# u's products over four token tiles, xh and xl in the place of x tiles 9 to 12

## The chip, the cores and the metric

The kernel runs on one core of a Trainium2 chip. A core has five engines that run beside each other and wait for each other by semaphores: TensorE (PE; its weight loads are shown apart as PEld), VectorE (DVE), ScalarE (ACT), GpSimd (POOL) and SyncE (SP), which here only issues transfers. Transfers run on the core's DMA engines, whichever queue issued them. The metric is the device time of one execution in microseconds, as the median of several runs.

## The reference

Two branches over the same x (2048 tokens of 640 values) are mixed with a gate per token.

```python
g = _sigmoid((x * gate_w).sum(-1, keepdims=True))
# branch A: y = Real(DFT_seq(DFT_hidden(x))), with the matrices as inputs
a = jnp.einsum("bsd,ed->bse", x, dft_hid_re)
b = jnp.einsum("bsd,ed->bse", x, dft_hid_im)
y = jnp.einsum("ts,bse->bte", dft_seq_re, a) - jnp.einsum("ts,bse->bte", dft_seq_im, b)
# branch B: 32 heads pick 2 of 256 experts each, by two lists of 16 scores
q = jnp.einsum("nd,dhc->nhc", xf, w_q)           # w_q: 640 x 32 x 256
s1 = jnp.einsum("nhd,ed->nhe", q[..., :dk], k1)  # and s2 with k2
...                                              # top 2 of each, top 2 of the 4 sums, softmax g
act = _gelu(jnp.einsum("nd,nhkd->nhk", xf, u[top_e]))
out = jnp.einsum("nhk,nhk,nhkd->nd", g, act, v[top_e])
return g_token * y + (1 - g_token) * out
```

## The kernel before, in words

Branch B's gathers are done as dense products: GELU(x u^T) for all 256 rows of u and all tokens, and a matrix of gate weights, expert by token, that is multiplied onto it before the product with v. Keys and w_q are multiplied into one score matrix first (WU holds it, and u behind it). Every fp32 operand is split into a high and a low part (`split`: ScalarE rounds to the high part, VectorE or GpSimd subtracts), and every product is three matmuls (`mm3`, lines 143 to 145: high by high, high by low, low by high).

**Pieces.** The sequence products of branch A are 128 pieces (`seq_piece`): real and imaginary part (w), four chunks of 512 columns (c), 16 token tiles (s). A piece is 15 matmuls: x tile s, split (tile X[s]), by five column blocks, against a 128x512 piece of the DFT matrix, into banks 0 to 4. wf is the loaded piece, WS its split ring of four; loads go out five pieces ahead and splits three. After a chunk's 16 pieces, ScalarE copies the banks to ST (line 246), VectorE multiplies by the token gate (line 217), and the partial goes to DRAM (pd, line 227).

**What stands between the pieces.** A table `then`, filled by `at(n, f)`, lists what follows piece n; the program is written out piece by piece, so this table sets the order on all engines and queues. In pieces 0 to 29 w_q is loaded in 32 loads (`load_wq`, five buffers), multiplied by the keys (`w_part`, line 365) and split. The first partial's stores follow piece 24 (`store_piece`, ScalarE's queue).

**Score steps.** From N0 = 30 on, tokens are taken in eight pairs of token tiles, p = 0 to 7, four `score_step`s each, one between two pieces. xT, loaded into xf, is split into xh and xl (`split_xT`); `sum_xT` forms four sums in place on VectorE (lines 437 to 440), split in `split_sums_xT`. Step 0 makes A (six matmuls, bank 5), then `u_pair` multiplies u by the pair's 256 tokens (30 matmuls of 256 columns, bank 7) and ScalarE takes the GELU into act (line 729), stored at once by SP (line 731). Then ScalarE copies A into bank 7 (Z), and step 1, one piece later, adds products onto it. VectorE finds top scores from `sc` in the background (`topk`, `gates`): a pump emits its instructions in proportion to TensorE's time.

**x tiles.** All 16 split x tiles (640 KB each) stay on chip in phase one. Tiles 0 to 8 are then written to DRAM (xd; `put_x`, AWAY = 9) and fetched for each chunk (`get_x`) during the score steps, into the places of tiles 6 to 8; from piece N1 = 66 on they come back to their own. Behind piece 127 stands the last part, hidden-dimension products with `raw` buffers taken from freed places.

Of the kernel before, what the change touches and what calls it, by code (L numbers as in the profile page):

```python
# [38 lines left out]
KZ = KD + 1  # L39
NSTEP = 7 * KZ  # L40
AHEAD = 5
AWAY = 9
BYPASS = 4
ACCUM_END = NT * (NC + 2) - 4

# [61 lines left out]
def gated_mix_kernel(ctx: ExitStack, tc: tile.TileContext, xT, xn, dreT, dimT, wsre, wsim, wq, kT, uT, vv, gw, out):  # L107
# [20 lines left out]
    def ps_t(shape, dt=F32):  # L128
        return bank(7, shape, dt)
# [6 lines left out]
    def split(f, h, l, eng):  # L136

        nc.scalar.activation(h, f, AF.Copy)  # L138
        eng.tensor_sub(l, f, h.bitcast(F32))  # L139
# [56 lines left out]
    def at(n, f, *args):  # L196
        then.setdefault(n, []).append(lambda: f(*args))
# [63 lines left out]
    p1 = p1_stack.enter_context(tc.tile_pool(name="p1", bufs=1, reuse_waits="tile"))  # L261
    pools = [p1]

    def load_x(s):
        if s < NT:
# [4 lines left out]
    def split_x(s):  # L270

        if s < NT:
            X[s] = big.tile([P, 2, D], F32R, name="X", tag=f"X{s}")
# [32 lines left out]


    warm = nc.const_aps.tensor(1.0, [P, 2 * P], mybir.dt.bfloat16)
    t = ps_t([P, 2 * P])
    for n in range(WARM):  # L310
        nc.tensor.matmul(t, warm[:, :P], warm, start=True, stop=True)  # L311

    split_x(0)
    load_piece(4)
# [105 lines left out]
    def split_xT(p, n):  # L420

        if p < NP:
            if not xs:
                xs.update((t, big.tile([P, 2, KD, P], F32R, name=t, tag=t)) for t in ("xh", "xl"))
            split(xf[p][:, n], xs["xh"][:, n], xs["xl"][:, n], nc.gpsimd)

    SX = {}

# [21 lines left out]
        nc.sync.dma_start(xd[s], X[s].bitcast(F32))  # L450

    def get_x(s, tag):
        X[s] = big.tile([P, 2, D], F32R, name="X", tag=f"X{tag}")
        nc.sync.dma_start(X[s].bitcast(F32), xd[s])

    for s in range(AWAY):
# [73 lines left out]
    def x_part(n, k0, k1):  # L530
        return [[xs[t][:, n, k] for k in range(k0, k1)] for t in ("xh", "xl")]

    def s_part(n):
        return [[t[:, k * P:(k + 1) * P] for k in range(2)] for t in SX[n]]
# [9 lines left out]
    def score_step(p, a):  # L544


        i0, i1 = 2 * p, 2 * p + 1
        copy = lambda o, f: nc.scalar.activation(o, f, AF.Copy)  # L548
        if a == 0:
            AB["A"] = bank(5)  # L550
            products(AB["A"], (x_part(0, 0, 2), w_part2(0, 2, 0)), first=True)
            split_sums_xT(p)
            u_pair(p)
            AB["Z"] = bank(7)
            copy(AB["Z"], AB["A"])
        elif a == 1:
            products(AB["Z"], (x_part(0, 2, 4), w_part2(2, 4, 0)), (x_part(0, 4, 5), w_part2(4, 5, 0)))
            new_sc(i0)
            copy(sc_half(i0, 0), AB["Z"])
            AB["Y"] = bank(6)  # L560
            products(AB["Y"], (s_part(1), t_part(1)), first=True)
            AB["Z"] = bank(7)
            copy(AB["Z"], AB["Y"])
            load_xT(p + 1)
        elif a == 2:
            products(AB["A"], (s_part(2), t_part(2)))
            copy(sc_half(i0, 1), AB["A"])
            products(AB["Z"], (s_part(4), w_part2(2, 4, 1)), (x_part(0, 4, 5), w_part2(4, 5, 1)))
            nc.vector.tensor_add(sc_half(i0, 1), sc_half(i0, 1), AB["Z"])
            bg.credit -= 0.75  # L570
            picks(i0, scs.pop(i0))
            products(AB["A"], (s_part(3), t_part(3)))
            new_sc(i1)
            copy(sc_half(i1, 1), AB["A"])
            split_xT(p + 1, 0)
        else:
            products(AB["Y"], (x_part(1, 4, 5), w_part2(4, 5, 1)))
            nc.vector.tensor_add(sc_half(i1, 1), sc_half(i1, 1), AB["Y"])
            products(AB["A"], (x_part(1, 2, 4), t_part(4)), (x_part(1, 4, 5), w_part2(4, 5, 0)))
# [137 lines left out]
        if i % NB == NB - 1:  # L717
            bg.add(gates(i // NB))

    def u_pair(p):  # L720
        xh, xl = xs["xh"], xs["xl"]
        ps = bank(7, (P, 2, 2 * P))
        for n in range(2):
            c = slice(n * P, (n + 1) * P)
# [4 lines left out]
        nc.scalar.activation(act, ps, AF.Gelu_apprx_tanh)  # L729
# [184 lines left out]
    def split_sums(k):  # L914
        if k == KD:
            f = p3.tile([P, 4 * TC], F32R, name="ts", tag="hot0")
            TS[8] = f[:, :2 * D]
            raw_free.append(f[:, 2 * D:2 * D + TC].bitcast(F32))
            raw_tags.extend((("xf", 2), ("X9", 2)))
        for n in () if k == KD else [k] + ([5 + k // 2] if k % 2 == 0 else []):  # L920
            TS[n] = big.tile([P, 2 * D], F32R, name="ts", tag=f"X{(1, 3, 4, 5, 6, 0, 2, 7)[n]}")
        t = T["t"]
        t1, t5, t3, t6 = (t[:, n * 2 * P:(n + 1) * 2 * P] for n in range(4))
        for n, f in enumerate((t1, t3, t5, t6, t[:, 8 * P:])):
            split(f, t_sum(k, n, 0), t_sum(k, n, 1), nc.gpsimd if n < 2 else nc.vector)
        bg.credit -= 1.0

    def load_v():
        T[KD] = big.tile([P, 2, D], F32, name="dt", tag="X9")
        nc.sync.dma_start(T[KD], vv.rearrange("k p d -> p k d"))  # L930

    def split_v():
# [13 lines left out]
    at(NPC + 14, store_gates, 1)  # L946


    fresh, raw_free = deque(), deque()
    raw_tags = [("X8", 2)] + [("wf", 1)] * 4 + [("X10", 2), ("wf", 1)] + [(f"X{s}", 2) for s in range(11, 16)]  # L950
    raw, sp = {}, {}

    def take(key):
# [305 lines left out]
```

## Time and profile before

| | |
|---|---|
| median of 3 runs | 752.96 us (752.92 to 755.22) |
| the profiled execution | 753.44 us, span 751.7 us |
| TensorE busy | 746.7 us, 4045 matmuls |
| VectorE, ScalarE, GpSimd busy | 587.4, 361.7, 346.6 us |
| granted TensorE clock | 1.000 |
| moved by DMA | 165.89 MB |

Busy time of an engine is the union of its instructions; matmuls overlap, so their pace is read from the starts of successive ones and not from their durations. In the timeline a row is start, duration, engine, line, operation, output and inputs; "x4" merges four, and what stands in brackets is the idle time before it and what ended it. A piece takes 3.40 us of TensorE.

### The profile page before, as it was taken

Reading aid. Unit: us, or ns where it says so; the run is one execution under the profiler, and the core shown is the slowest. Engines: PE = TensorE matmul, PEld = TensorE weight load, DVE = VectorE, ACT = ScalarE, POOL = GpSimd, SP = SyncE. Lnnn points to the kernel's source line nnn. Section 1 sums busy time; section 2 is a strip of 40 time slices with the busy share of each in tenths; the row PEclk is TensorE's granted clock in tenths of the full one; section 3 lists DMA queues with packets and bytes.
Section 4 is the critical chain, followed back from the end, with each engine's and each line's share of the span. In section 5 each row is a group of like instructions: output and inputs, shape, how many; then the busy total and the mean of one; then the engine's idle time right before and its main releaser. Section 6 shows DMA issues by size and latency. Waiting matters only on the chain.

```text
span 751.7 us, 11366 instructions
## 1 busy us (share of the span) xinstructions
PE 746.7 (99%) x4045; PEld 610.7 (81%) x4045; DVE 587.4 (78%) x741; ACT 361.7 (48%) x660; POOL 346.6 (46%) x286
## 2 busy tenths in 40 slices
PE   9999999999999999999999999999999999999998
PEld 7777777888888888888888888888888888888887
DVE  6864088278999999998999888979999983357651
ACT  4334134534345835553734687633555653443451
POOL 5533225342424424334345445643356793487253
PEclk9999999999999999999999999999999999999999
DMA  9999999478366786663496856388766689775301
GB/s 334 378 388 356 342 381 345 132 191 278 57 174 149 184 273 164 159 167 118 121 376 210 175 146 203 116 255 291 264 225 209 218 261 335 228 233 182 112 29 71
DMA packets 84490, 165.89 MB, mean 221 GB/s; under 512 B 16081, under 2 KB 23377, under 8 KB 84177
## 3 DMA queue, kind: packets, MB, share of 16 engines
q1 hardware_dynamic: 70960, 140.89, 55.5%
q0 software_dynamic: 5472, 9.96, 8.6%
q10 hardware_dynamic: 8000, 14.31, 5.2%
q8 instruction: 32, 0.52, 0.3%
q14 instruction: 26, 0.20, 0.1%
HBM read 132.46 MB, written 31.08 MB: 218 GB/s over the span
## 4 chain that ended last, share of the span: by engine, by line
PE 96%; DMA 2%; DVE 2%; issue 0%; SPq 0%; ACT 0%
PE b L143 30%; PE b L144 30%; PE b L145 30%; PE b L239 2%; PE b L365 2%; DMA wq<-in_wq 2%; PE b L815 1%; PE b L311 1%; DVE ST L217 1%; DVE WU L139 0%; DVE tw L139 0%; DVE wp L371 0%; ACT WU L138 0%; DVE tt L397 0%; DVE tt L396 0%
## 5 line engine op out<-in xcount | busy, mean ns | idle before, releaser
L143 PE MATMUL b<-WS,X 128*128 128x512 f32 x620 | 243.5, 393 | 0.0
L144 PE MATMUL b<-WS,X 128*128 128x512 f32 x620 | 241.5, 389 | 0.0
L145 PE MATMUL b<-WS,X 128*128 128x512 f32 x620 | 241.3, 389 | 0.0
L139 POOL TENSOR_TENSOR WS<-wf,WS 128x512 fp32r<-128x512 f32 x89 | 135.9, 1532 | 162.8 <-ACT WS L138 157.9
L143 PEld LDWEIGHTS b<-WS,X 128*128 128x128 f32 x620 | 116.4, 188 | 28.0 <-issue 4.1
L145 PEld LDWEIGHTS b<-WS,X 128*128 128x128 f32 x620 | 116.4, 188 | 24.5
L144 PEld LDWEIGHTS b<-WS,X 128*128 128x128 f32 x620 | 116.4, 188 | 23.3
L138 ACT ACTIVATE WS<-wf 128x512 fp32r<-128x512 f32 x89 | 55.7, 629 | 76.9 <-PE b L145 32.1
L803 DVE TENSOR_TENSOR hot<-rows,wtab 128x1024 f16<-128x1024 f16 x64 | 62.7, 1005 | 0.7 <-PE b L815 0.6
L139 POOL TENSOR_TENSOR WS<-ra,WS 128x512 fp32r<-128x512 f32 x39 | 55.1, 1426 | 15.3 <-ACT WS L138 13.2
L139 POOL TENSOR_TENSOR xl<-xf,xh 128x640 fp32r<-128x640 f32 x16 | 28.2, 1767 | 69.3 <-ACT xh L138 62.9
L138 ACT ACTIVATE WS<-ra 128x512 fp32r<-128x512 f32 x55 | 34.5, 631 | 50.9 <-PE b L145 36.0
L548 ACT ACTIVATE sc<-b 128x512 f32<-128x512 f32 x32 | 19.2, 600 | 80.7 <-PE b L145 80.7
L191 POOL DMA_DIRECT2D WS<-in_wsre x30 | 26.4, 880 | 68.0 <-ACT WS L189 66.6
L773 ACT ACTIVATE b<-b,mask 128x128 f32<-128x128 f32 x128 | 43.0, 342 | 13.5 <-PE b L815 10.4
L139 POOL TENSOR_TENSOR WP<-ra,WP 128x512 fp32r<-128x512 f32 x18 | 26.4, 1482 | 43.2 <-ACT WP L138 43.1
L598 DVE TENSOR_TENSOR eq<-sc,mm 128x1024 f16<-128x1024 f32 x32 | 41.4, 1293 | 0.9
L605 DVE TENSOR_REDUCE tied<-eq 128x64 f32<-128x1024 f16 x32 | 39.0, 1219 | 0.9
L596 DVE TENSOR_REDUCE mm<-sc 128x64 f32<-128x1024 f32 x32 | 38.8, 1212 | 0.3
L217 DVE SCALAR_TENSOR_TENSOR ST<-ST,grow 128x512 f32<-128x512 f32 x40 | 31.4, 846 | 0.6 <-ACT ST L246 0.6
L143 PE MATMUL b<-WU,xh 128*128 128x512 f32 x80 | 31.2, 391 | 0.0
L145 PE MATMUL b<-WU,xl 128*128 128x512 f32 x80 | 31.1, 389 | 0.0
(203 smaller groups left out, 1468.8 us busy)
## 6 DMA issues: line engine op xcount, KB each, us to landing
wq<-in_wq SPq DMA_DIRECT2D x32, 640.0 KB, 7.1
X<-xd SPq DMA_DIRECT2D x30, 640.0 KB, 6.6
wf<-in_wsim SPq DMA_DIRECT2D x64, 256.0 KB, 4.8
wf<-in_wsre SPq DMA_DIRECT2D x63, 256.0 KB, 6.5
ra<-pd SPq DMA_DIRECT2D x47, 256.0 KB, 3.7
pd<-ST ACTq DMA_DIRECT2D x35, 256.0 KB, 5.2
WS<-in_wsre POOLq DMA_DIRECT2D x30, 256.0 KB, 5.3
xd<-X SPq DMA_DIRECT2D x9, 640.0 KB, 9.4
```

Of the source, the lines that this page charges most:

```text
L138: nc.scalar.activation(h, f, AF.Copy)
L139: eng.tensor_sub(l, f, h.bitcast(F32))
L143: nc.tensor.matmul(o, wh, ah, start=first, stop=False, skip_group_check=more)
L144: nc.tensor.matmul(o, wh, al, start=False, stop=False, skip_group_check=more)
L145: nc.tensor.matmul(o, wl, ah, start=False, stop=last, skip_group_check=more)
L191: nc.gpsimd.dma_start(l, (wsre, wsim)[w][c, s], accum_op=OP.add)
L217: nc.vector.scalar_tensor_tensor(f, f, -1.0 if w else 1.0, g, op0=OP.mult, op1=OP.mult)
L596: nc.vector.tensor_reduce(m, sc, op=OP.max, axis=AX.X)
L598: nc.vector.tensor_tensor(eq, sc, m[:, :, None].to_broadcast([P, HH, E]), op=OP.is_equal)
L605: nc.vector.tensor_reduce(tied[:, s, ib, :], eq, op=OP.add, axis=AX.X)
L773: nc.scalar.activation(f[:, :, n], f[:, :, n], AF.Copy, scale=mask4[:, n:n + 1])
L803: nc.vector.tensor_tensor(o, a, b, op=op)
```

## The change

u's products no longer stand in each pair but in the odd ones (1, 3, 5, 7), for the 512 tokens of two pairs (`u_pairs`): 512 columns per matmul, first half of u's rows into bank 7, second into bank 6. Each half gets its own GELU and its own buffer (`put_act`; act, and a part of ROWS[1] or of the place of xf), and both are stored at the beginning of the next step (`store_acts`). xh and xl hold two pairs, in the places of x tiles 9, 10 and 11, 12. So tiles 9 and 10 also go to DRAM (AWAY = 11; stored behind wq's loads at piece 25) and come back, and tiles 11 and 12 are copied by ScalarE into the old places of xh and xl and back (`move_x`). The free pieces without a score step move: they stood ahead of pairs 2, 4 and 6 and stand ahead of pairs 1, 3 and 5. The first partial's stores move from piece 24 to 28, `load_dd` by one and two pieces, and buffers of the last part come from other places. The last warm-up matmul writes another part of its bank.

TensorE, around the first score step of pair 0 (b5 is A, b7 u's products, b0 and b1 the next piece), before:

```order
L145 MATMUL b5_1279<-WU_86,xl_1111 128x512
L143 MATMUL b7_1294<-xh_1110,WU_86 128x256
L144 MATMUL b7_1294<-xl_1111,WU_86 128x256
L145 MATMUL b7_1294<-xh_1110,WU_86 128x256
L143 MATMUL b7_1294<-xh_1110,WU_86 128x256
```

and in the changed kernel at the same place, and below it the beginning of u's products in pair 1:

```order
L145 MATMUL b5_1283<-WU_86,xl_1156 128x512
L143 MATMUL b0_1300<-WS_90,X_1128 128x512
L144 MATMUL b0_1300<-WS_90,X_1128 128x512
L145 MATMUL b0_1300<-WS_90,X_1128 128x512
L143 MATMUL b1_1301<-WS_90,X_1128 128x512
```
```order
L145 MATMUL b5_1506<-WU_86,xl_1156 128x512
L143 MATMUL b7_1522<-xh_1155,WU_86 128x512
L144 MATMUL b7_1522<-xl_1156,WU_86 128x512
L145 MATMUL b7_1522<-xh_1155,WU_86 128x512
L143 MATMUL b7_1522<-xh_1155,WU_86 128x512
```

In pair 0 the next piece follows A at once; in pair 1 u's products stand there with 512 columns.

ScalarE's queue at the end of wq's loads (pd00 is the first partial, wf a piece, uf a part of u, xf the first pair's xT), before:

```order
L138 ACTIVATE WS_90<-wf_904 128x512
L227 DMA pd00_69<-ST_68 128x512 x5
L138 ACTIVATE tw_924<-tt_1003 128x2x128
L138 ACTIVATE tw_926<-tt_1003 128x2x128
L138 ACTIVATE tw_928<-tt_1003 128x2x128
```

and now, four pieces further on:

```order
L138 ACTIVATE WU_86<-uf_1071 128x256
L138 ACTIVATE xh_1155<-xf_901 128x640 x2
L138 ACTIVATE WS_90<-wf_1073 128x512
L227 DMA pd00_69<-ST_68 128x512 x5
L138 ACTIVATE tw_926<-tt_1187 128x2x128
```

The five stores stand behind the first split of xT instead of two pieces ahead of wq's last loads.

VectorE, ahead of pair 4's sums of xT (xf), before:

```order
L578 TENSOR_TENSOR sc_2189<-sc_2189,b6_2119 128x512
L605 TENSOR_REDUCE tied_1937<-eq_2187 128x64
L596 TENSOR_REDUCE mm_1936<-sc_2117 128x64
L437 TENSOR_TENSOR xf_2129<-xf_2129 128x256
L438 TENSOR_TENSOR xf_2129<-xf_2129 128x256
```

and now:

```order
L627 TENSOR_TENSOR eq_2154<-eq_2154,powers_159 128x1024
L217 SCALAR_TENSOR_TENSOR ST_68<-ST_68,grow_2067 128x512 x5
L602 TENSOR_TENSOR sc_2156<-sc_2156,b6_2087 128x512
L452 TENSOR_TENSOR xf_2098<-xf_2098 128x256
L453 TENSOR_TENSOR xf_2098<-xf_2098 128x256
```

The third partial's five gate products, which stood behind the sums, stand ahead of them.

```diff
-AWAY = 9
+AWAY = 11
...
-            at(n + (8 if q == 0 else 1), store_piece, q)
+            at(n + (12 if q == 0 else 1), store_piece, q)
...
+    def place(tag):
+        if tag in (9, 11):
+            TWIN[tag] = big.tile([P, 2, 2, D], F32R, name="X", tag=f"X{tag}")
+        if tag in (9, 10, 11, 12):
+            return TWIN[tag - (tag + 1) % 2][:, (tag + 1) % 2]
+        return big.tile([P, 2, D], F32R, name="X", tag=f"X{tag}" if isinstance(tag, int) else tag)
+
+    def move_x(s, tag):
+        old, X[s] = X[s], place(tag)
+        nc.scalar.activation(X[s], old.bitcast(F32), AF.Copy)
...
-                xs.update((t, big.tile([P, 2, KD, P], F32R, name=t, tag=t)) for t in ("xh", "xl"))
+                xs.update((t, big.tile([P, 2, 2, KD, P], F32R, name=t, tag=tag)) for t, tag in (("xh", "X9"), ("xl", "X11")))
...
+    for s, tag in ((11, "xh"), (12, "xl")):
+        at(s + 5, move_x, s, tag)
...
+    for s in range(9, AWAY):
+        at(b - 2, put_x, s)
...
-        at(n - 3, split_xT, 0, a)
+        at(n - 2, split_xT, 0, a)
...
             split_sums_xT(p)
-            u_pair(p)
+            if p % 2:
+                u_pairs(p // 2)
             AB["Z"] = bank(7)
             copy(AB["Z"], AB["A"])
+            if p % 2:
+                put_act(p // 2, 1)
         elif a == 1:
+            if p % 2:
+                store_acts(p // 2)
...
-            for k in range(KD):
-                mm3(ps[:, n, :], UH[:, k, c], UL[:, k, c], xh[:, :, k, :], xl[:, :, k, :], k == 0 and n == 0, k == KD - 1, True)
-            run_bg(1.8)
-        act = p2.tile([P, 2, 2 * P], F32, name="act")
-        nc.scalar.activation(act, ps, AF.Gelu_apprx_tanh)
-        for n in range(2):
-            nc.sync.dma_start(actd[n][:, 2 * p * P:2 * (p + 1) * P], act[:, n])
+            AB["u", n] = ps = bank(7 - n)
+            for k in range(KD):
+                mm3(ps, UH[:, k, e], UL[:, k, e], xh[:, :, :, k, :], xl[:, :, :, k, :], k == 0, k == KD - 1)
+                run_bg(0.68)
+            if n == 0:
+                put_act(c, 0)
...
+    def store_acts(c):
+        for n in range(2):
+            nc.sync.dma_start(actd[n][:, c * TC:(c + 1) * TC], AB.pop(("act", n)))
...
-        n = N0 + 4 * p + p // 2
+        n = N0 + 4 * p + min((p + 1) // 2, 3)
...
+    for s in (11, 12):
+        at(N1, move_x, s, s)
...
-        at(N1 + 4 + 2 * m, load_dd, m)
+        at(N1 + 5 + 3 * m, load_dd, m)
```

More of the change, by code (lines that the diff above doesn't have):

```diff
@@ L272, in split_x @@
         if s < NT:
-            X[s] = big.tile([P, 2, D], F32R, name="X", tag=f"X{s}")
+            X[s] = place(s)
             f = xr[s // 2][:, s % 2]
@@ L308, in gated_mix_kernel @@
     warm = nc.const_aps.tensor(1.0, [P, 2 * P], mybir.dt.bfloat16)
-    t = ps_t([P, 2 * P])
+    t = ps_t([P, TC])
     for n in range(WARM):
-        nc.tensor.matmul(t, warm[:, :P], warm, start=True, stop=True)
+        c = slice(0, 2 * P) if n < WARM - 1 else slice(2 * P, TC)
+        nc.tensor.matmul(t[:, c], warm[:, :P], warm, start=n < WARM - 1, stop=True, skip_group_check=n == WARM - 1)
     split_x(0)
@@ L452, in get_x @@
     def get_x(s, tag):
-        X[s] = big.tile([P, 2, D], F32R, name="X", tag=f"X{tag}")
+        X[s] = place(tag)
         nc.sync.dma_start(X[s].bitcast(F32), xd[s])
-    for s in range(AWAY):
+    for s in range(9):
         at(6 + 2 * s, put_x, s)
@@ L528, in products, with x_part @@
             run_bg(0.68)
-    def x_part(n, k0, k1):
-        return [[xs[t][:, n, k] for k in range(k0, k1)] for t in ("xh", "xl")]
+    def x_part(p, n, k0, k1):
+        return [[xs[t][:, p % 2, n, k] for k in range(k0, k1)] for t in ("xh", "xl")]
     def s_part(n):
@@ L567, in score_step @@
             copy(sc_half(i0, 1), AB["A"])
-            products(AB["Z"], (s_part(4), w_part2(2, 4, 1)), (x_part(0, 4, 5), w_part2(4, 5, 1)))
+            products(AB["Z"], (s_part(4), w_part2(2, 4, 1)), (x_part(p, 0, 4, 5), w_part2(4, 5, 1)))
             nc.vector.tensor_add(sc_half(i0, 1), sc_half(i0, 1), AB["Z"])
@@ L718, in picks, with put_act, u_pairs @@
             bg.add(gates(i // NB))
-    def u_pair(p):
+    def put_act(c, n):
+        if n == 0:
+            f = p2.tile([P, TC], F32, name="act")
+        elif c < NC - 1:
+            f = ROWS[1].rearrange("p a b c -> p (a b c)").bitcast(F32)[:, :TC]
+        else:
+            f = big.tile([P, TC], F32, name="act", tag="xf")
+        nc.scalar.activation(f, AB.pop(("u", n)), AF.Gelu_apprx_tanh)
+        AB["act", n] = f
+    def store_acts(c):
+        for n in range(2):
+            nc.sync.dma_start(actd[n][:, c * TC:(c + 1) * TC], AB.pop(("act", n)))
+    def u_pairs(c):
         xh, xl = xs["xh"], xs["xl"]
-        ps = bank(7, (P, 2, 2 * P))
         for n in range(2):
-            c = slice(n * P, (n + 1) * P)
+            e = slice(n * P, (n + 1) * P)
+            AB["u", n] = ps = bank(7 - n)
             for k in range(KD):
-                mm3(ps[:, n, :], UH[:, k, c], UL[:, k, c], xh[:, :, k, :], xl[:, :, k, :], k == 0 and n == 0, k == KD - 1, True)
-            run_bg(1.8)
-        act = p2.tile([P, 2, 2 * P], F32, name="act")
-        nc.scalar.activation(act, ps, AF.Gelu_apprx_tanh)
-        for n in range(2):
-            nc.sync.dma_start(actd[n][:, 2 * p * P:2 * (p + 1) * P], act[:, n])
+                mm3(ps, UH[:, k, e], UL[:, k, e], xh[:, :, :, k, :], xl[:, :, :, k, :], k == 0, k == KD - 1)
+                run_bg(0.68)
+            if n == 0:
+                put_act(c, 0)
     for p in range(NP):
-        n = N0 + 4 * p + p // 2
+        n = N0 + 4 * p + min((p + 1) // 2, 3)
         for a in range(4):
@@ L917, in split_sums @@
             TS[8] = f[:, :2 * D]
-            raw_free.append(f[:, 2 * D:2 * D + TC].bitcast(F32))
-            raw_tags.extend((("xf", 2), ("X9", 2)))
+            raw_free.extend(LENT[0][:, a * TC:(a + 1) * TC] for a in range(2))
+            raw_tags.append(("xf", 2))
         for n in () if k == KD else [k] + ([5 + k // 2] if k % 2 == 0 else []):
@@ L928, in load_v @@
     def load_v():
-        T[KD] = big.tile([P, 2, D], F32, name="dt", tag="X9")
+        f = big.tile([P, 2, 2, D], F32, name="dt", tag="X9")
+        T[KD], f = f[:, 0], f[:, 1].rearrange("p k d -> p (k d)")
+        fresh.extend(f[:, a * TC:(a + 1) * TC] for a in range(2))
+        LENT.append(T[KD].rearrange("p k d -> p (k d)"))
         nc.sync.dma_start(T[KD], vv.rearrange("k p d -> p k d"))
@@ L946, in gated_mix_kernel @@
     at(NPC + 14, store_gates, 1)
-    fresh, raw_free = deque(), deque()
-    raw_tags = [("X8", 2)] + [("wf", 1)] * 4 + [("X10", 2), ("wf", 1)] + [(f"X{s}", 2) for s in range(11, 16)]
+    LENT, fresh, raw_free = [], deque(), deque()
+    raw_tags = [("X8", 2)] + [("wf", 1)] * 5 + [("X11", 5)] + [(f"X{s}", 2) for s in range(13, 16)]
     raw, sp = {}, {}
```

11 lines of the change are left out of this document (6 added, 5 removed).

## The prediction

> **What bounds the kernel now.** I read the page first (engines, then the chain that ended last), then what TensorE waited for, then the timeline at the places that the change touches.
>
> ```profile
> span 751.7 us, 11366 instructions
> PE 746.7 (99%) x4045; PEld 610.7 (81%) x4045; DVE 587.4 (78%) x741; ACT 361.7 (48%) x660; POOL 346.6 (46%) x286
> PE 96%; DMA 2%; DVE 2%; issue 0%; SPq 0%; ACT 0%
> ```
> ```profile
> PE b L365 <- DMA wq<-in_wq: 0.8, 2, 0.6
> PE b L311 <- PEq L1251: 0.8, 1, 0.8
> ```
> TensorE is busy 99% of the span, it is 96% of the chain, and it waits for nothing but the start and two loads of wq. So time comes from three things only: how many matmuls there are and at which pace, the few pauses that exist, and pauses that the change may open. Work on other engines costs nothing as long as TensorE doesn't wait for it.
>
> **u's products.** Busy times overlap, so I take the pace from starts in the timeline of the first pair.
>
> ```profile
> L145 PE MATMUL b<-xh,WU 128*128 128x256 f32 x80 | 22.6, 283 | 0.0
> ```
> ```profile
> 136.95 0.28 PE L143 MATMUL b<-xh,WU 128*128 128x256 f32 x1
> ...
> 140.54 0.40 PE L143 MATMUL b<-WS,X 128*128 128x512 f32 x1
> ...
> 143.97 0.39 PE L143 MATMUL b<-WU,xh 128*128 128x512 f32 x1
> ...
> 147.37 0.39 PE L143 MATMUL b<-WS,X 128*128 128x512 f32 x1
> ...
> 150.77 0.39 PE L143 MATMUL b<-tw 128*128 128x512 f32 x1
> ```
> The first row is one of the three lines of `mm3`: 3 x 80 = 240 matmuls of 256 columns, 30 in each of eight pairs. A pair's 30 take 140.54 - 136.95 = 3.59 us. The piece of 15 wide matmuls behind them takes 143.97 - 140.54 = 3.43, the next piece 150.77 - 147.37 = 3.40, so the narrow run also slows its successor by 0.03. Before: 8 x (3.59 + 0.03) = 28.96 us. After: the same columns in 120 matmuls of 512, at 3.40 / 15 = 0.2267 each = 27.20 us. **Gain 1.76 us**; at the slower 3.43 / 15 it would be 1.5, so the bounds are 1.5 and 1.8. A narrow one costs 0.1197, which is 6 ns more than half of a wide one: a fixed 13 ns for each matmul, and 120 of them go.
>
> The Trainium skill, "TensorE: Matmul & The Clock Gate", section "Back-to-back issue gap", gives a warm gap of columns / 2.4 GHz plus 2.5 ns. By that rule a removed matmul saves 2.5 ns, u's gain is an estimated 0.3 us, and the sum below would end 1.46 us later, at 751.6. The rows say about 13 ns for this stream, which loads new weights for each matmul, and a time worked out from them is what I use.
>
> **The pause in the last pair.** TensorE and then ScalarE, last pair (u's products end with the matmul at 356.84):
>
> ```profile
> 360.16 0.39 PE L145 MATMUL b<-WS,X 128*128 128x512 f32 x1
> 360.52 0.50 PE L143 MATMUL b<-WU,xh 128*128 128x512 f32 x1
> 360.86 0.40 PE L144 MATMUL b<-WU,xh 128*128 128x512 f32 x1
> ```
> ```profile
> 357.22 0.72 ACT L138 ACTIVATE h<-xf 128x256 fp32r<-128x256 f32 x2 [0.46 <-DVE xf L440]
> 357.96 1.28 ACT L729 ACT_TABLE_LOAD   x1
> 359.26 0.60 ACT L729 ACTIVATE act<-b 128x512 f32<-128x512 f32 x1
> 359.89 0.58 ACT L548 ACTIVATE b<-b 128x512 f32<-128x512 f32 x1
> ```
> The next products add to bank 7, which ScalarE fills with A's copy at 359.89 to 360.47, behind the sums' splits, the table load and the GELU. Two steps of 0.36 and 0.34 stand where 0.227 is the pace: 0.24 us lost. In the changed order the last pair has 30 matmuls of 512 columns between A and those products, 6.8 us instead of 3.59, and only the first half's GELU stands before the copy. I take the **0.24 us as gained** (bounds 0 and 0.24).
>
> **The two waits for wq.** A group without a wait, and the two with one:
>
> ```profile
> 80.21 2.29 PE b L365 x32
> 114.24 6.88 DMA wq<-in_wq
> ```
> ```profile
> 105.56 1.82 PE L365 MATMUL b<-wq,kp 128*32 128x320 f32 x24
> 108.28 0.50 PE L143 MATMUL b<-WS,X 128*128 128x512 f32 x1
> 118.72 1.82 PE L365 MATMUL b<-wq,kp 128*32 128x320 f32 x24
> 121.85 0.50 PE L143 MATMUL b<-WS,X 128*128 128x512 f32 x1
> ```
> ```profile
> 98.65 5.23 SPq L356 DMA_DIRECT2D wq<-in_wq  x2
> 111.48 0.91 SPq L356 DMA_DIRECT2D wq<-in_wq  x2
> 113.36 0.33 SPq L406 DMA_DIRECT2D uf<-in_uT  x1
> 105.08 3.49 ACTq L227 DMA_DIRECT2D pd<-ST  x4
> 105.80 1.50 DVE L139 TENSOR_TENSOR WU<-uf,WU 128x256 fp32r<-128x256 f32 x1
> ```
> The group at 105.56 takes 2.72 instead of 2.29 (0.43 lost), that at 118.72 takes 3.13 (0.84 lost, its last load lands at 114.24 + 6.88 = 121.12). Between them ScalarE's queue issues the first partial's five stores (one and the four shown, 256 KB each, 1.3 MB). The change moves them four pieces back, to piece 28, so they no longer compete with the last five wq loads, nor hold ScalarE's queue for 3.5 us. The last load is still issued near 114.2, because SP reaches it only behind the uf load at 113.36. But the two loads of 111.48 and 111.90 stand on SP behind an earlier uf load, whose buffer VectorE frees at 107.30, and TensorE frees theirs by 107; with ScalarE's stores out of the way they go out at about 108, three microseconds and more sooner. The last one is needed when the 24 matmuls ahead of it are through, 118.72 + 1.82 = 120.5, that is 6.3 us after its issue instead of 6.88; 0.6 us must be saved, and 1.3 MB that stood ahead of it have gone. I take the second wait as gone, **0.84 us**, bounds 0 and 0.84. The first belongs to a load issued at 98.65, six us ahead of the stores: I leave it at 0.43 (gain bounds 0 and 0.43).
>
> **What moves in its place, costed at nothing.** Prices and lead times:
>
> ```profile
> GB/s 334 378 388 356 342 381 345 132 191 278 57 174 149 184 273 164 159 167 118 121 376 210 175 146 203 116 255 291 264 225 209 218 261 335 228 233 182 112 29 71
> X<-xd SPq DMA_DIRECT2D x30, 640.0 KB, 6.6
> pd<-ST ACTq DMA_DIRECT2D x35, 256.0 KB, 5.2
> ```
> ```profile
> 119.19 1.35 ACT L138 ACTIVATE xh<-xf 128x640 fp32r<-128x640 f32 x2
> 133.64 2.75 ACT L246 ACTIVATE ST<-b 128x512 f32<-128x512 f32 x5
> ```
> - The stores of x tiles 9 and 10 (1.3 MB) follow wq's last load on SP. At the 345 GB/s of that slice they put 3.8 us before every later load, about what the moved partial gives back. xh and xl now lie where those tiles were, so the split at 119.19 waits for the stores to land, to about 122; TensorE needs it four pieces after 121.85, at 135.5. Cover about 8 us after the split itself and GpSimd's half.
> - The partial's stores, issued at about 124 to 126, land about 6 us later; ST is rewritten from 133.64 on, five copies in bank order, and TensorE needs bank 0 again after piece 31 (135.5) and A (1.36). Cover 2 to 4 us; beyond that each microsecond late costs one.
> - Six more reads of 640 KB (tiles 9 and 10 in pieces 41, 42, 57, 58 and back in 73, 74). Each goes out three pieces ahead, with two pieces (6.8 us) and at least two score steps as cover against 6.6.
> - Four copies on ScalarE of 128x1280: two 128x640 take 1.35, so 1.35 each, on an engine that is 48% busy and splits three pieces ahead. The GELUs stay eight, 128x512 each; their stores become eight of 256 KB, and SP reaches them when the values are there. `load_dd` is one and two pieces later; what it loads is multiplied only after piece 127.
>
> Sum: 1.76 + 0.24 + 0.84 = 2.84 us. The profiled execution took 753.44 us (span 751.7 and 1.7 around it), which gives 750.60; it stood 0.48 over the median 752.96, and the forecast for the median is **750.1**.
>
> **Rivals.**
> *Even pairs lose their cover* (the slower side). In pairs 2, 4 and 6 (counted from 0 to 7) no u stands between A and the products that need A's copy; one piece does. The chain is: last product of the pair before, split of xT, VectorE's four sums, ScalarE's four splits, the copy.
>
> ```profile
> 190.88 0.39 PE L145 MATMUL b<-WU,xl 128*128 128x512 f32 x1
> 348.38 0.39 PE L145 MATMUL b<-WU,xl 128*128 128x512 f32 x1
> ```
> ```profile
> 194.22 0.43 DVE L437 TENSOR_TENSOR xf<-xf 128x256 f32<-128x256 f32 x1 [1.03 <-POOL xl L139]
> 354.91 0.42 DVE L437 TENSOR_TENSOR xf<-xf 128x256 f32<-128x256 f32 x1
> ```
> ```profile
> 196.52 0.71 ACT L138 ACTIVATE h<-xf 128x256 fp32r<-128x256 f32 x2
> ```
> ```profile
> 259.78 4.19 DVE L217 SCALAR_TENSOR_TENSOR ST<-ST,grow 128x512 f32<-128x512 f32 x5
> ```
> From the product at 190.88 the splits end at 197.23, the copy (0.58) at about +6.95. TensorE arrives after the rest of that product, a piece, six products and a piece: 0.23 + 3.40 + 1.36 + 3.40 = 8.39. Slack 1.4 us. At 348.38 VectorE was late (354.91, +6.53, no idle time before it): splits end at 357.94, copy at +10.2. With that lag each of the three pairs pauses 1.8, together 5.4: 755.5. It decides from a lag of VectorE's first sum above +4.7 (a pause begins) and of +6.4 in all three (the kernel is slower by 0.3%). For it: pair 4's sums now stand behind five ST products, 4.19 in the row. Against it: the batch sums that made VectorE late now stand ahead of odd pairs' sums, which keep 6.8 us of u as cover. Milder, one or two pauses of 0.5 to 1: about 751.5.
> *The second wq wait stays*, because SP gets past uf no earlier and the last load queues behind the others: 752.96 - 2.0 = 750.96.
> *Late partial stores*: if they land 5 us later than I think, TensorE waits some 3 us at piece 32: 753.1; further stretched, up to 755.5.
> *The fixed cost isn't saved* (the wide stream paces as if only 2.5 ns went): 751.6; no row bears it out.
>
> **How the numbers follow.** A difference under 0.3% (2.26 us, so 750.70 to 755.22) can't be told from none. Chances: forecast 0.55; the wq wait stays 0.18; small pauses in even pairs or at piece 32, 0.14; no saving of the fixed cost 0.02; pauses in even pairs at the last pair's lag 0.07; a longer one at the stores or elsewhere 0.04. So faster 0.55, same 0.34, slower 0.11. The range: below, all bounds at once, 1.8 + 0.24 + 0.84 + 0.43 = 3.3, rounded down to 749.5; above, the forecast with 2.4 us of new pauses, 752.5.
>
> **What would show it.** u's 120 matmuls start 0.227 apart and number 40 for each line of `mm3`; the group of the last wq loads takes 2.29, with TensorE's waits naming wq at most once; no step over 0.34 in the last pair; between A's piece and the products on bank 7 in pairs 2, 4 and 6 no gap. The prediction is wrong if TensorE waits for the copy on ScalarE, for ST's rewriting at 133, or for an X tile.

## The result, and the profile after

| | before | changed |
|---|---|---|
| median of 6 runs each | 753.61 us (752.92 to 755.22) | 750.85 us (750.43 to 751.62) |
| ratio | | 0.9962, 95% interval 0.9948 to 0.9975 |
| the profiled execution | 753.44 us, span 751.7 | 750.43 us, span 748.7 |
| TensorE busy | 746.7 us, 4045 matmuls | 743.8 us, 3925 matmuls |

The medians differ by 2.76 us, 0.37%; the forecast was 2.84. By the interval of the ratio the gain lies between 1.9 and 3.9 us. Two later comparisons of the same two kernels gave ratios of 0.9955 (0.9943 to 0.9967) and 0.9964 (0.9951 to 0.9977).

The page of the changed kernel (span, first engine line, chain) and what TensorE waited for:

```profile
span 748.7 us, 11141 instructions
PE 743.8 (99%) x3925; PEld 603.8 (81%) x3925; DVE 585.7 (78%) x741; ACT 365.9 (49%) x664; POOL 342.4 (46%) x286
PE 94%; DMA 5%; SPq 0%; DVE 0%; ACT 0%; issue 0%; ACTq 0%
```
```profile
PE b L326 <- PEq L1296: 0.8, 1, 0.8
PE b L380 <- DMA wq<-in_wq: 0.7, 1, 0.7
```

TensorE is as full as it was, and still waits for nothing but the start and wq. It names wq once, not twice. (L326 and L380 are lines 311 and 365 of before.)

u's products, first of the four runs, from the timeline of TensorE, the last row being the piece behind; below it the group of the third line of `mm3`:

```profile
165.10 0.39 PE L143 MATMUL b<-xh,WU 128*128 128x512 f32 x1
...
171.90 0.39 PE L143 MATMUL b<-WS,X 128*128 128x512 f32 x1
```
```profile
L145 PE MATMUL b<-xh,WU 128*128 128x512 f32 x40 | 15.6, 389 | 0.0
```

30 matmuls take 171.90 - 165.10 = 6.80 us, 0.2267 each, and there are 40 for each line.

The last two groups on wq:

```profile
104.86 1.82 PE L380 MATMUL b<-wq,kp 128*32 128x320 f32 x24
107.37 0.74 PE L380 MATMUL b<-wq,kp 128*32 128x320 f32 x8 [0.69 <-DMA wq<-in_wq]
108.05 0.50 PE L143 MATMUL b<-WS,X 128*128 128x512 f32 x1
...
118.48 2.36 PE L380 MATMUL b<-wq,kp 128*32 128x320 f32 x32
120.77 0.50 PE L143 MATMUL b<-WS,X 128*128 128x512 f32 x1
```

The second group runs through in 120.77 - 118.48 = 2.29 us. The first takes 108.05 - 104.86 = 3.19, so about 0.9 is lost where before lost 0.43.

Where do the 3.0 us between the two profiled executions lie? Three stretches, by the starts of TensorE's matmuls: up to the first group on wq (29.29 before, 28.59 after: 0.70 gained); from there to the first wide matmul behind the last such group (121.85 and 120.77: 92.56 and 92.18, 0.38 gained); from there to the first group of the expert part (422.65 and 419.64: 300.80 and 298.87, 1.93 gained). Behind that, 329.0 us are left in both. The first was in no forecast, the second was forecast as 0.84 and the third as 2.00. To see which of this belongs to the change, here are the same places in every profile but those of a_lag and a_put21, two experiments below that put waits of several microseconds between them:

| run | first wq group starts | lost at 105 | lost at 118 | wide matmul behind the last group | from there to the expert part |
|---|---|---|---|---|---|
| before | 29.29 | 0.43 | 0.83 | 121.85 | 300.80 |
| b_again (before) | 29.07 | 0.18 | 0.92 | 121.45 | 300.86 |
| b_st28 | 29.06 | 0.24 | 0 | 120.59 | 300.81 |
| changed | 28.59 | 0.89 | 0 | 120.77 | 298.87 |
| a_again (changed) | 29.07 | 0.07 (and 0.63 at 54) | 0 | 121.11 | 298.87 |
| a_again2 (changed) | 29.50 | 1.21 | 0.23 | 122.26 | 298.86 |
| a_st24 | 28.51 | 0 | 2.19 | 121.98 | 298.90 |
| a_narrow | 29.05 | 0.93 | 0 | 121.27 | 300.53 |
| a_free_old | 28.74 | 0 (and 0.21 at 54) | 0.78 | 121.03 | 299.94 |
| a_st30 | 29.60 | 0.25 | 0 | 121.14 | 299.44 |
| a_put8 | 29.64 | 0 | 0 | 120.93 | 299.90 |
| a_put8b | 28.80 | 0 | 1.54 | 121.62 | 298.90 |

The last column is the same to 0.06 us wherever the code is the same: 300.8 before, 298.9 after. The columns ahead of it scatter for one and the same code: in the three profiles of the changed kernel the start by 0.91, the loss at 105 by 1.14 and the wide matmul by 1.49 us.

### The profile page after: what moved, and what is told of

Read it like the earlier page. It is cut to its first block, busy times and chain, and to the rows that moved or that the text cites. A ratio compares the mean times of both kernels' runs of the same rounds, so it can differ in the third digit from the quotient of the medians.

```text
span 748.7 us, 11141 instructions
## 1 busy us (share of the span) xinstructions
PE 743.8 (99%) x3925; PEld 603.8 (81%) x3925; DVE 585.7 (78%) x741; ACT 365.9 (49%) x664; POOL 342.4 (46%) x286
## 4 chain that ended last, share of the span: by engine, by line
PE 94%; DMA 5%; SPq 0%; DVE 0%; ACT 0%; issue 0%; ACTq 0%
PE b L143 30%; PE b L145 30%; PE b L144 30%; PE b L239 2%; DMA wf<-in_wsre 2%; PE b L380 2%; DMA wq<-in_wq 1%; PE b L857 1%; DMA xd<-X 1%; DMA gdr<-gc 1%; DVE wp L386 0%; SPq L177 0%; ACT WS L295 0%; ACTq L514 0%; DVE ST L1191 0%
## 5 line engine op out<-in xcount | busy, mean ns | idle before, releaser
L139 POOL TENSOR_TENSOR WS<-wf,WS 128x512 fp32r<-128x512 f32 x89 | 131.9, 1486 | 168.3 <-ACT WS L138 151.8
L845 DVE TENSOR_TENSOR hot<-rows,wtab 128x1024 f16<-128x1024 f16 x64 | 57.8, 930 | 4.3 <-PE b L857 4.3
L139 POOL TENSOR_TENSOR WS<-ra,WS 128x512 fp32r<-128x512 f32 x33 | 47.1, 1439 | 14.3 <-ACT WS L138 14.1
L138 ACT ACTIVATE WS<-ra 128x512 fp32r<-128x512 f32 x47 | 29.4, 631 | 42.4 <-PE b L145 29.6
L622 DVE TENSOR_TENSOR eq<-sc,mm 128x1024 f16<-128x1024 f32 x32 | 44.4, 1387 | 0.9
L139 POOL TENSOR_TENSOR WP<-ra,WP 128x512 fp32r<-128x512 f32 x13 | 19.2, 1490 | 31.0 <-ACT WP L138 30.9
L845 DVE TENSOR_TENSOR hot<-hot,rows 128x1024 f16<-128x1024 f16 x32 | 31.6, 986 | 0.0
```

What stands on the lines that cost most here:

```text
L622: nc.vector.tensor_tensor(eq, sc, m[:, :, None].to_broadcast([P, HH, E]), op=OP.is_equal)
L845: nc.vector.tensor_tensor(o, a, b, op=op)
```

## The experiments

### The start: before, once more

The kernel before against itself, no edit.

> The kernel before, unchanged, against itself. In the profile of before TensorE's first group on wq begins at 29.30, in that of after at 28.61, because the warm-up matmuls reach the short pace (0.11 us instead of 0.21) only after piece 0 has begun in the one and at 3.5 us in the other. Theory (the start is chance, not the change): this profile may begin its first wq group anywhere between 28.6 and 29.5, and the group on wq near 105 waits the longer the earlier TensorE arrives (0.41 at 29.30, 0.87 at 28.61, landing of the last load at 107.3 to 107.6 in each). The group near 118.5 again waits about 0.8. Rival (the start belongs to the kernel): 29.30 again. Time ratio 1.000 within 0.2%.

753.60 us, ratio 1.0002 (0.9990 to 1.0013); 11 runs from 752.06 to 756.35. The start came at 29.07, and in the changed kernel it came at 28.59, 29.07 and 29.50 in three profiles. So the 0.70 us at the start are chance and not the change. Where they come from, in the timelines of TensorE (before, and changed; the third profile, a_again2, has a row like the first):

```profile
0.77 4.21 PE L311 MATMUL b<-const-bfloat16-1.0 128*128 128x256 bf16 x19 [0.77 <-PEq L1251]
```
```profile
0.77 3.66 PE L326 MATMUL b<-const-bfloat16-1.0 128*128 128x256 bf16 x19 [0.77 <-PEq L1296]
```

The 19 warm-up matmuls begin at 0.77 in each. In the second row the step between two of them falls from 0.213 to 0.11 us at 3.7 us; in the other two profiles it stays at 0.213 to the end, and the first matmuls of piece 0 still run at about half pace (in a_again2 one step of 0.574 and three of 0.427 instead of 0.227, until about 6.5 us). The Trainium skill, "TensorE: Matmul & The Clock Gate", section "What's actually happening", says that the array's clock doubles after a busy window of about 3.4 us that runs freely and doesn't begin with the kernel, so that the point varies by some 500 ns to either side. The traces agree that it varies, by more. The view of busy times shows a granted clock of 1.00 over these microseconds in both, because the trace's record of the clock has no entry ahead of the change; its first entry, at full clock, stands at 5.93, 3.68 and 6.52 us in the three, and anywhere from 3.68 to 6.77 over all fourteen profiles, those of before at 5.46 to 5.93 among them. The first wq group follows it: from 28.74 with the change at 4.84 to 29.64 with the change at 6.77, half a microsecond for each.

That the group near 105 waits the longer the earlier TensorE arrives, as expected above, the table doesn't bear out: the earliest start (28.51) lost nothing there, and a late one (29.50) lost 1.21.

### The first partial's stores: that part alone, and that part undone

```diff
-            at(n + (8 if q == 0 else 1), store_piece, q)
+            at(n + (12 if q == 0 else 1), store_piece, q)
```

put into the kernel before (b_st28):

> The kernel before with one part of the change: the first partial's stores follow piece 28 instead of 24. Theory (those stores hold the last wq loads back): the group near 118.5 takes 2.29 instead of 3.13, its wait is gone, the group near 105.5 is unchanged, nothing waits near 135: 0.8 us less than before, ratio 0.9989. Rival (SP gets to the last load no earlier, because it stands behind the uf load): the wait stays at 0.8, ratio 1.000.

and taken back in the changed kernel (a_st24):

> The changed kernel with that one part undone: the first partial's stores back behind piece 24. Theory: the group near 118.5 waits again, by 0.8 or more since the stores of x tiles 9 and 10 now follow on SP; ratio 0.9962 + 0.0011 = 0.9973, about 0.8 us over the changed kernel. Rival (the wait went for another reason, such as the earlier start): it stays gone and the time is that of the changed kernel, 0.9962.

b_st28: 752.70 us, ratio 0.9990 (0.9981 to 0.9998), 0.63 under the median of before beside it (0.15 to 1.4 by the interval). The groups on wq in its profile:

```profile
105.34 2.61 PE L365 MATMUL b<-wq,kp 128*32 128x320 f32 x32
118.30 2.36 PE L365 MATMUL b<-wq,kp 128*32 128x320 f32 x32
```

a_st24: 751.68 us, ratio 0.9984 (0.9969 to 0.9998), 0.83 over the changed kernel's median where 0.8 was expected; the intervals of the two ratios overlap, so the trace has to show the rest. The second group:

```profile
117.50 1.82 PE L380 MATMUL b<-wq,kp 128*32 128x320 f32 x24
121.31 0.75 PE L380 MATMUL b<-wq,kp 128*32 128x320 f32 x8 [1.98 <-DMA wq<-in_wq]
```

The wait goes with the stores and comes back with them, in either kernel. It comes back as 2.19 us and not 0.84, because this execution arrived early (no loss at 105) and the load landed at 121.27, where it landed in before too (121.13): TensorE reached that group at 117.50 here and at 118.72 there, and the landing didn't follow. But the stores aren't all of it. With them behind piece 24 the last load took 6.7 to 7.7 us in three profiles; with them at 28 or 30 it took 4.8 to 5.2 in eight, and 6.4 to 7.1 in three (a_again2, a_free_old, a_put8b), and there the table shows the wait again.

In the table the three profiles with the stores behind piece 24 reach the wide matmul at 121.76 in the mean; the eight with the stores at 28 or 30 and nothing else moved ahead of it (not the same eight: b_st28, the changed kernel three times, a_narrow, a_free_old, a_st30, and a_lag below with 120.33) at 121.06. The move is worth 0.70 us by that, 0.63 by b_st28's time. Since the eight alone spread from 120.33 to 122.26, either number is rough.

### u's matmuls at half width, in the same places

```diff
-                mm3(ps, UH[:, k, e], UL[:, k, e], xh[:, :, :, k, :], xl[:, :, :, k, :], k == 0, k == KD - 1)
+                for h in range(2):
+                    hs = slice(2 * P * h, 2 * P * (h + 1))
+                    mm3(ps[:, hs], UH[:, k, e], UL[:, k, e], xh[:, h, :, k, :], xl[:, h, :, k, :], k == 0 and h == 0, k == KD - 1, True)
```

> The changed kernel with each of u's 120 matmuls of 512 columns done as two of 256, in the same places: 60 narrow ones in each odd pair, 240 in all. Theory (a fixed 13 ns for each matmul of this stream): a pair's run takes 60 x 0.1197 = 7.18 instead of 6.80 us, 4 x 0.38 + 4 x 0.03 for the matmul behind, 1.6 to 1.76 us more: ratio 0.9962 + 0.0022 = 0.9984. Rival (2.5 ns each): 0.3 us more, ratio 0.9966.

752.59 us, ratio 0.9988 (0.9979 to 0.9997): 1.74 over the changed kernel's median. In the table's last column it costs 300.53 - 298.87 = 1.66 us, with four narrow runs; before had eight, and at 0.03 each for the slower successor that is 1.78 for the change. That column repeats to 0.06 us, so 13 ns for each matmul of this stream holds; 2.5 ns would have shown 0.3.

### Stores in the way of wq's loads

The store of x tile 8 stands on SP just ahead of the load that TensorE waits for at 105. Moved behind the stores of tiles 9 and 10 (a_put8):

```diff
-    for s in range(9):
+    for s in range(8):
         at(6 + 2 * s, put_x, s)
...
     for s in range(9, AWAY):
         at(b - 2, put_x, s)
+    at(b - 1, put_x, 8)
```

beside the changed kernel again (a_again):

> The changed kernel, unchanged, beside the next ones. In the six profiles so far TensorE's first wq group begins between 28.51 and 29.29, and the group near 105 then waits 0.2 to 0.9 (0 once). Theory (its seventh group waits for transfers that have been at the limit since the start): an early start is partly given back there, so the time moves less than the start does. The second wait stays gone. Ratio 0.9962 (750.4 to 751.0).

> The changed kernel with the store of x tile 8 moved from piece 22, where it is issued at 96.55 just ahead of the wq load that TensorE waits for (97.25 to 107.33), to piece 26, behind the stores of tiles 9 and 10. Theory (the first wq wait is the transfers' limit): 640 KB less ahead of that load, at about 360 GB/s 1.8 us; it lands near 105.5, the wait of 0.87 goes, the last wq load lands at about 118.6 as before against a need at 117.6 + 1.8, so no wait comes back: 0.4 to 0.9 us less than the changed kernel, about 750.2, ratio 0.9953. Rival (the load is held by its buffer or its queue, not by the stream): it lands at 107.3 again, and the time stays.

a_again took 750.76 us, a_put8 750.49, ratio 0.9956 (0.9942 to 0.9969). The load landed at 105.81 and no wait was left at 105, as the theory says (a_st30, which started at nearly the same time, had that load at 107.70; a_again lost only 0.07 there, so the times alone don't show it). There was no wait at 118 either. But time was lost further on; ScalarE's and TensorE's waits, and the place:

```profile
ACT WS L188 <- DMA wf<-in_wsre: 3.1, 1, 3.1
```
```profile
135.79 0.39 PE L145 MATMUL b<-WU,xl 128*128 128x512 f32 x1
136.61 0.50 PE L143 MATMUL b<-WS,X 128*128 128x512 f32 x1 [0.43 <-ACT ST L246]
```

The store at piece 26 held up SP's later loads (x tile 2, which goes to the place of tile 8, was issued at 130.34 instead of 125.86). A piece came late, ScalarE waited 3.1 us for it, and behind that split stood the copies that free the banks: 0.59 us at 136 and 0.23 at 140.

So the store was moved by one piece only, behind two wq loads (a_put8b):

```diff
-        at(6 + 2 * s, put_x, s)
+        at(6 + 2 * s + (s == 8), put_x, s)
```

> The changed kernel with the store of x tile 8 moved from piece 22 only to piece 23, behind the two wq loads issued at 97.25 and 98.92 and not in front of them, and still four pieces ahead of the first load into the place of tile 6. Theory (the first wq wait is the transfers' limit; moved to piece 26 the store held up SP's later loads, ScalarE's split waited 3.1 us for one of them and TensorE 0.6 for the copies behind it): the load of 97.25 lands 1.8 us sooner, near 105.5, the waits for wq are gone, and no pause comes at 135: 0.3 to 0.9 us less than the changed kernel, about 750.2. Rival (what is gained ahead of 107 comes back as a wait further on, whatever the place): the median stays within 0.3 us of the changed kernel.

Beside the changed kernel once more:

> The changed kernel, unchanged, beside the next three. By the runs so far: 750.4 to 751.0, ratio 0.996; TensorE's first wq group begins anywhere between 28.5 and 29.6; the waits for wq together are 0 to 0.9.

a_put8b took 750.74 us, ratio 0.9960 (0.9944 to 0.9975), a_again2 751.07 (0.9964): not to be told apart. The first wait went again (landed 104.62), and the second came back in its place:

```profile
105.08 2.36 PE L380 MATMUL b<-wq,kp 128*32 128x320 f32 x32
117.79 1.82 PE L380 MATMUL b<-wq,kp 128*32 128x320 f32 x24
120.95 0.74 PE L380 MATMUL b<-wq,kp 128*32 128x320 f32 x8 [1.34 <-DMA wq<-in_wq]
```

The chain of its waits, in order of time, up to that group:

```profile
112.44 0.43 DVE WU L139
...
112.89 0.33 SPq L421
...
113.78 7.12 DMA wq<-in_wq
...
120.95 0.74 PE b L380 x8
```

VectorE's split of u frees a buffer, SP issues the uf load that waited for it, and only then wq's last load. This load is issued at 113.5 to 114.7 in every profile but a_put21's (115.61), while the end of TensorE's group ahead of it moves from 107.07 to 109.28. So the rival's time holds: the median stays within 0.3 us of the changed kernel. Its reason, that what is gained ahead of 107 is waited for at 118, rests on this one profile, in which the last load took 7.12 us. With the 5.2 us that it took at most in the eight profiles without a wait there it would have landed at 118.98, an estimate, ahead of the need at 117.79 + 1.82 = 119.61; and a_put8 had no wait at either place. No version was found that beats the changed kernel by more than the comparisons can tell.

The opposite: the stores of tiles 9 and 10 ahead of the wq loads (a_put21).

```diff
     for s in range(9, AWAY):
-        at(b - 2, put_x, s)
+        at(b - 6, put_x, s)
```

> The changed kernel with the stores of x tiles 9 and 10 at piece 21 instead of 25, ahead of the last eleven wq loads. Theory (transfers are at their limit up to 107): 1.31 MB more ahead of the load that TensorE waits for, 3.6 us at 360 GB/s; the group near 105 waits 3.6 us more than in the changed kernel (0 to 0.9 there), the group near 118 not, and the time is 2.5 to 3.6 us longer: 753.3 to 754.4. Rival (five wq buffers and idle stretches of the queues take it up): under 1 us longer.

755.57 us, ratio 1.0020 (1.0007 to 1.0034), 4.5 over the changed kernel beside it: more than either expectation. The timeline of TensorE and, for 112 to 116 us, the row of busy times (after the engines: granted clock, DMA share, GB/s):

```profile
111.11 0.75 PE L380 MATMUL b<-wq,kp 128*32 128x320 f32 x8 [3.71 <-DMA wq<-in_wq]
111.79 0.78 PE L143 MATMUL b<-WS,X 128*128 128x512 f32 x1
...
115.31 0.39 PE L145 MATMUL b<-WS,X 128*128 128x512 f32 x1
```
```profile
112.00:116.00 4.00, 4.00 (x11) 3.18 (x12) 3.17 (x7) 1.65 (x4) 1.28 (x1) 0.59 0.94 362
```

The wait is 3.9 us in all, as the limit of the transfers says (1.31 MB at 360 GB/s is 3.6). Behind it eight matmuls take 115.31 - 111.79 = 3.52 us instead of 1.81 at a granted clock of 0.59: another 1.7 us. Of these 5.6 us the changed kernel itself loses 0.1 to 1.2 at 105. The section of the Trainium skill named above says that an idle window of about 3.4 us halves the clock until a busy one has passed. This trace agrees in the length: its record of the clock has half clock from 111.83 to 115.25, 3.41 us. It begins 0.72 us after the matmuls have resumed, and 111.83 - 6.02 = 105.81 us behind the change to full clock at the start, which is 31 times 3.413. Of the 3.41 us ahead of it TensorE was idle for 2.69, so in this case it wasn't idle to its end.

### Free pieces where they were

```diff
-        n = N0 + 4 * p + min((p + 1) // 2, 3)
+        n = N0 + 4 * p + p // 2
```

> The changed kernel with the free pieces where they were, ahead of pairs 2, 4 and 6 instead of 1, 3 and 5, so that odd pairs come a piece earlier. In the changed kernel A's copy ends 1.53, 1.05 and 1.94 us ahead of the products that need it in pairs 2, 4 and 6, and 5.4 us ahead in odd pairs behind u. Theory: no pair pauses in either order, the time is that of the changed kernel within 0.2 us. Rival (the free piece ahead of odd pairs hides the split of xT, xl on GpSimd ends 1 to 2 us ahead of A): with a piece less TensorE waits up to 2 us in each of three pairs, 752 to 756.

751.76 us, ratio 0.9969 (0.9957 to 0.9980), 1.0 over a_again, though the two intervals overlap. No pair pauses, so the rival is out; but the time didn't stay within 0.2 us. Its profile shows one pause in another place, the last piece ahead of the first expert group. GpSimd's queue loads a part of its split:

```profile
408.04 0.89 POOL L191 DMA_DIRECT2D WS<-in_wsim  x1 [1.56 <-ACT WS L189]
```
```profile
416.29 0.39 PE L143 MATMUL b<-WS,X 128*128 128x512 f32 x1
417.55 0.50 PE L144 MATMUL b<-WS,X 128*128 128x512 f32 x1 [0.88 <-DMA WS<-in_wsim]
```

This load took 9.46 us to land; in the changed kernel, issued at 407.91, it took 7.58 and was in place 0.7 us ahead of its matmul. In a_free_old SP had issued two of the loads that share the time, a piece and a row of gates, ahead of it, and in the changed kernel behind it. Whether that is why it came late was not tried, nor whether a second profile of this order shows it.

### The partial's stores still later

```diff
-            at(n + (12 if q == 0 else 1), store_piece, q)
+            at(n + (14 if q == 0 else 1), store_piece, q)
```

> The changed kernel with the first partial's stores behind piece 30 instead of 28. In the changed kernel they land at 129.22 to 134.53 and TensorE needs banks 0 to 4 again from 135.86 to 138.6. Theory (late stores hold ST, ST holds the banks): two pieces later they land 6.8 us later, at 136.0 to 141.3, and the last bank is free at 141.9 instead of 138.6: TensorE pauses up to 3.3 us, 2 to 3.3 in all: 753 to 754. Rival (the stores are quicker there, since less else is under way): under 1 us.

750.85 us, ratio 0.9961 (0.9947 to 0.9974): no difference from a_again. The theory's price was wrong: the stores landed at 135.06 to 137.64 and not at 136.0 to 141.3, 4.5 to 5.1 us after their issue. Less was under way by then: 311 GB/s from 130 to 136 us, where the changed kernel moved 401 from 122 to 134. ScalarE's copies followed each landing, and TensorE lost 0.45 us at 140 and 0.11 behind it:

```profile
140.08 0.50 PE L143 MATMUL b<-WU,xh 128*128 128x512 f32 x1 [0.28 <-ACT b L567]
```

### VectorE made late ahead of the even pairs

```diff
+            if p in (2, 4, 6):
+                for n in range(3):
+                    for t in range(2):
+                        nc.vector.tensor_scalar(f[:, t], f[:, t], 1.0, None, op0=OP.mult)
             nc.vector.tensor_add(a22, a21, a22)
```

> The changed kernel with VectorE made late on purpose ahead of the sums of xT in pairs 2, 4 and 6: six products of xf by 1.0 in place, 128x640 each, which change no value. Theory (the slower rival of the forecast, with its price): with these six taking D us together, each of the three pairs pauses by D less its slack in the changed kernel (1.53, 1.05, 1.94 us), so at D = 2.1 us 0.57 + 1.05 + 0.16 = 1.8 us, at D = 4.2 us 2.67 + 3.15 + 2.26 = 8.1 us. Rival (other work, such as the split on GpSimd, ends the wait, and VectorE's lag is hidden): no pause.

First the slack in the changed kernel, pairs 2, 4 and 6: ScalarE's copy of A, and the first product that needs it.

```profile
199.03 0.58 ACT L567 ACTIVATE b<-b 128x512 f32<-128x512 f32 x1
...
261.52 0.58 ACT L567 ACTIVATE b<-b 128x512 f32<-128x512 f32 x1
...
322.52 0.58 ACT L567 ACTIVATE b<-b 128x512 f32<-128x512 f32 x1
```
```profile
201.14 0.39 PE L143 MATMUL b<-WU,xh 128*128 128x512 f32 x1
...
263.15 0.39 PE L143 MATMUL b<-WU,xh 128*128 128x512 f32 x1
...
325.03 0.39 PE L143 MATMUL b<-WU,xh 128*128 128x512 f32 x1
```

The same products in a_lag:

```profile
201.67 0.50 PE L143 MATMUL b<-WU,xh 128*128 128x512 f32 x1 [0.81 <-ACT b L571]
...
265.94 0.50 PE L143 MATMUL b<-WU,xh 128*128 128x512 f32 x1 [1.99 <-ACT b L571]
...
328.93 0.50 PE L143 MATMUL b<-WU,xh 128*128 128x512 f32 x1 [0.81 <-ACT b L571]
```

759.14 us, ratio 1.0070 (1.0043 to 1.0098), with runs from 756.44 to 761.87. The pause comes where the rival of the forecast had it. VectorE's first sum starts 5.78, 6.97 and 5.79 us behind the last product of the pair before (3.34, 3.80 and 3.35 in the changed kernel), and the pauses, as steps over 0.227, are 0.97, 2.15 and 0.98: it begins at a lag of 4.8 in all three. The six products took 2.5 to 3.5 us (D) and moved the first sum by 2.44, 3.17 and 2.44; less the slack that gives 0.91, 2.12 and 0.50, so pair 6 pauses by 0.5 more than the theory says. The three with their slower successors make 4.4 us of the profiled run, which was the shortest; the last pair adds 0.6, and at the first expert group TensorE waits 0.9 for VectorE. What the longer runs add was not profiled; the two longest have a mean granted clock of 0.998 and 0.996, the others 1.000.

## Why the prediction was right

**u's products.** Forecast 1.76; measured 1.78 by a_narrow with the 0.03 counted, a pace of 6.80 / 30. The rule of 2.5 ns, rival of 751.6, is out for this stream. (The section of the Trainium skill that the prediction cites for it gives it as the gap of an isolated matmul.)

**The pause in the last pair.** Forecast 0.24, and the two long steps of 0.246 together are gone. As the prediction says, ScalarE's copy is now through 2.8 us before the products that need it (the first row is ScalarE's copy, the second the first of these products):

```profile
354.26 0.58 ACT L567 ACTIVATE b<-b 128x512 f32<-128x512 f32 x1
```
```profile
357.67 0.39 PE L143 MATMUL b<-WU,xh 128*128 128x512 f32 x1
```

A step of 0.316 at 247.38, in pair 3, is new and was foreseen by nothing: 0.09 lost, in every profile of the changed kernel and its variants but a_free_old. The weight load of the matmul there waits 0.24 us for ScalarE's copy of scores, which took 0.97 us instead of 0.60:

```profile
247.35 0.19 PEld L143 LDWEIGHTS b<-tw,h 128*128 128x128 f32 x1 [0.24 <-ACT sc L567]
```

1.78 + 0.25 - 0.09 = 1.94 is the table's 300.8 against 298.9.

**The two waits for wq.** The mechanism of the second was right: with the stores out of the way two loads went out at 107.59 and 108.07 (forecast about 108), the last one still behind uf at 113.53, and it landed 5.1 us later. The step that was mis-sized is "0.84 and 0.43 left": the waits aren't two amounts that stand by themselves. What is lost at 118 hangs on when TensorE arrives and on how long the last load takes, which is issued between 113.5 and 114.7 whether TensorE is early or late; so the wait taken as gone was 0 in the profiled execution, but 0.23 in a_again2. What is lost at 105 was anything from 0.07 to 1.21 in the changed kernel's three profiles, with the load landing at 107.33 to 108.57; why it moves stays open. Transfers are at their limit up to there (busy share 1.02, 401 GB/s, from 90 to 107 us). Over the profiles the move is worth 0.6 to 0.7 us, a rough number as said above.

**What was costed at nothing.** The stores of tiles 9 and 10 landed at 120.36 and 122.08 (forecast: to about 122). The partial's stores were issued at 122.93 to 125.36, but took 6.3 to 9.2 us instead of 6; the last copy to ST waited 0.08 us for them, TensorE not at all. The six more reads, the four copies and the GELUs cost nothing that a row shows.

**Even pairs.** Slack forecast 1.4; measured 1.53, 1.05 and 1.94. Deciding lag forecast +4.7; measured 4.8. VectorE's lag was +3.3 to +3.8, so the slower side stayed away by about one microsecond.

**The sum.** 1.78 + 0.16 + 0.63 to 0.70 = 2.57 to 2.64 explained out of 2.76. The forecast of 750.1 stands 0.75 under the median; 0.65 of that is the base, since before's median over six runs is 753.61 and not 752.96. The start's chance alone moves the first wq group by up to 1.1 us. That the difference of the medians came within 0.08 of the forecast is luck, since its interval is 1.9 to 3.9; what is shown term by term is 1.8 for u, the pause of 0.25, and a gain at wq whose size is rough.

## What to carry to other kernels

On an engine that is busy 99%, removed instructions pay at the pace that the timeline shows for that very stream, here 13 ns for each matmul beyond its columns, and that gain arrived in full. A gain ahead of a wait for a transfer is less safe: where the issue of the load hangs on another engine (113.5 to 114.7 here, whenever TensorE came), time won ahead of it can turn into waiting, as it did in the profile of a_put8b. Before a difference under 0.3% is read from two profiles, profile the same code again; the parts of the span that scatter and the parts that don't can then be told apart.

## What the runs showed of the hardware

- TensorE's step from half to full pace at the start came between 3.7 and 6.8 us for the same 19 warm-up matmuls, and the first wq group began anywhere from 28.51 to 29.64 us.
- The changes of the granted clock lie on one grid: in each of the fourteen profiles the last change lies 218 to 220 times 3.413 us behind the first (before: 753.45 - 5.93 = 747.52 = 219 x 3.413).
- A wait of 3.7 us in the middle of a busy stream cost 1.7 us more in slow matmuls behind it; behind the waits of up to 2.0 us in the other profiles one step of 0.34 stood, and then the full pace of 0.227.
- wq's last load took 4.8 to 5.2 us in the eight profiles of the changed order and of b_st28 that had no wait at 118, and 6.4 to 7.1 in a_again2, a_free_old and a_put8b, with much the same transfers around it (a_again2 is the same kernel as a_again). What decides between them stays open.
